# Routing attention and hardswish FFN on one core: decode intermediates in a PSUM bank, two banks for short-lived results, checks later

## The chip, the cores and the metric

The kernel runs on one core of a Trainium2 chip. Five engines work side by side, each on its own queue in program order: TensorE (PE, matrix products, with its weight loads in a row of their own, PEld), VectorE (DVE), ScalarE (ACT), GpSimd (POOL) and SyncE (SP, which issues transfers). The metric is device time in microseconds for one execution. Before the change three runs gave a median of 1086.1 us (1086.04 to 1087.46).

## The reference

Attention over 4 batches of 8 heads, 768 positions, 64 numbers per head, in which a query sees only keys of its own cluster (of 16), and then a feed-forward block with a hardswish.

```python
q_assign = np.argmax(np.einsum('bhsd,hcd->bhsc', q_n, c_n), axis=-1)   # nearest centroid
k_assign = np.argmax(np.einsum('bhsd,hcd->bhsc', k_n, c_n), axis=-1)
mask = q_assign[:, :, :, None] == k_assign[:, :, None, :]
scores = np.where(mask, scale * q @ k.T, -1e9)
attn = softmax(scores) @ v                       # (4, 8, 768, 64)
x = attn.transpose(0, 2, 1, 3).reshape(3072, 512)
h = x @ w_in                                     # (3072, 2048)
out = (h * np.clip(h + 3, 0, 6) / 6) @ w_out     # (3072, 512)
```

`w_in` and `w_out` come as 64-bit floats. The kernel turns them into 32-bit floats itself, from their two 32-bit words, in 32 chunks of 128 x 512.

## The kernel before

All work goes pair by pair: 16 pairs of heads, 12 steps n for each, two steps at a time. r is the place of such a double step in its pair (0, 2, ..., 10). Its engines' queues hold the instructions in the order of this loop:

```python
for n in range(0, total + lag_d + 2, 2):          # total = 192, lag_d = 4
    g, r = divmod(n, per_pair)                    # per_pair = 12
    scores(n), scores(n + 1)                      # PE ps, ACT ex, POOL acc
    attn_v(n - 2), attn_v(n - 1)                  # PE pv; at the end of a half: ACT num
    for check in later:                           # range passes and counts of the last double step
        check()
    later.clear()
    m = n - lag_d + 1
    if m >= 0 and m % NCH == NCH - 1:             # NCH = 6: at r = 2 and r = 8
        later.append(divide(m))
    prep = prep_items(g + 1, r)                   # next pair: r = 0, 2: two turns; 4: cluster_scores;
                                                  # 6: route; 8: two route_turns; 10: one
    if r == 4 and prep:
        prep.pop()()
    if n == DECODED:                              # DECODED = 96
        st["early"] = False
    ...                                           # loads, FFN items, mixed with prep one by one
    for step in decode[: share[r]]:               # share = {0: 5, 2: 3, 4: 4, 6: 1, 8: 3, 10: 4}
        step()
    del decode[: share[r]]
    ...
    if n >= total:
        for check in later:
            check()
        later.clear()
```

Short-lived results of PE (transposes, cluster scores, denominators) go to PSUM through `scratch`. Of the eight banks, `ps` has four, `pv` one, the pool `psum_t` one and the pool `psum_m` two. Up to n = 96 two of three such tiles go to `psum_m`, which the FFN's products `ph` share, and the third to `psum_t`; from n = 96 all go to `psum_t`.

```python
def scratch(shape, name):
    st["scratch"] += 1
    if st["early"] and st["scratch"] % 3:
        return psum_m.tile(shape, F32, name=name, tag="m")
    return psum_t.tile(shape, F32, name=name, tag="t")

def turn(g, part):
    ...
    pt = scratch([P, NHC, P], "pqk")              # three transposes of q or k
    ...
    nc.scalar.copy(out=dst, in_=pt)               # xf

def route_turn(g, part):
    ...
    po = scratch([P, 4, P], "po")
    ...
    nc.scalar.copy(out=xm[:, part * 4 : part * 4 + 4], in_=po)

def divide(n):
    ...
    pd = scratch([P, 512], "pd")[:, 0:HALF]       # denominators, from POOL's acc
    ...
    nc.vector.reciprocal(out=rcp, in_=pd)
    nc.vector.tensor_tensor(out=st["xT", b][...], in0=num, in1=rcp, op=ALU.mult)
    return lambda: in_range(2 * g + hf, rcp)

def in_range(i, rcp):                             # two passes of ACT with sums
    nc.scalar.activation(out=rcp, in_=rcp, func=ACT.Copy, accum_out=totals[:, 0, i : i + 1])
    nc.scalar.activation(out=rcp, in_=rcp, func=ACT.Relu, bias=low_c, scale=-1.0,
                         accum_out=totals[:, 1, i : i + 1])
```

`route` compares the transposed cluster scores `pr` with their maxima `mx` on DVE, giving `one_hot`, and appends a `count` (two ACT passes over `one_hot`) to `later`. `cluster_scores` writes `pcs`, which ACT copies to `cs`.

A chunk of weights is decoded in five steps; `lo` and `hi` are the two words, interleaved in SBUF. The tiles `wsize`, `wtop` and `wunit` are in SBUF, each twice.

```python
def split():
    load_weights(i + 1)
    ...
    nc.scalar.activation(out=got["size"], in_=got["hi"].bitcast(F32), func=ACT.Abs, accum_out=...)
    nc.vector.tensor_scalar(out=got["top"], in0=got["hi"], scalar1=3, scalar2=0x3FFFFFFF,
        op0=ALU.logical_shift_left, op1=ALU.bitwise_and)                     # wtop<-raw
def join():
    nc.vector.scalar_tensor_tensor(out=got["top"], in0=got["hi"], scalar=0xC0000000, in1=got["top"],
        op0=ALU.bitwise_and, op1=ALU.bitwise_or)                             # wtop<-raw,wtop
def power():
    nc.scalar.activation(out=got["size"], in_=got["size"], func=ACT.Relu, ..., accum_out=...)
    nc.vector.tensor_scalar(out=got["unit"], in0=got["top"], scalar1=0xFF800000, scalar2=None,
        op0=ALU.bitwise_and)                                                 # wunit<-wtop
def rest():
    nc.vector.scalar_tensor_tensor(out=unit, in0=got["lo"], scalar=2.0**-52, in1=unit,
        op0=ALU.mult, op1=ALU.mult)                                          # wunit<-raw,wunit
def total():
    nc.vector.tensor_tensor(out=chunks[i][0], in0=got["top"].bitcast(F32),
        in1=got["unit"].bitcast(F32), op=ALU.add)                            # w_in_sb<-wtop,wunit
```

Of the kernel before, what the change touches and what calls it, by code (L numbers as in the profile page):

```python
# [10 lines left out]
U32 = mybir.dt.uint32  # L11
# [7 lines left out]
P = 128  # L19
# [10 lines left out]
WC = 512  # L30
# [86 lines left out]
def fast_path(ctx, tc, ok, q, k, v, centroids, moe_w_in, moe_w_out, out):  # L117
# [6 lines left out]
    def pool(name, bufs, **kw):  # L124
        return ctx.enter_context(tc.tile_pool(name=name, bufs=bufs, **kw))
# [14 lines left out]
    decp = decoding.enter_context(tc.tile_pool(name="decp", bufs=2))  # L140
    psum_s = pool("psum_s", 2, space=PSUM)
    psum_v = pool("psum_v", 1, space=PSUM)
    psum_t = pool("psum_t", 1, space=PSUM)
# [17 lines left out]
    counts = const.tile([P, 2, NPAIR], F32, name="counts")  # L161
    w_low = const.tile([P, 1], F32, name="w_low")

    st = {"scratch": 0}
    later = []

    def scratch(shape, name):

        st["scratch"] += 1
        if st["early"] and st["scratch"] % 3:  # L170
            return psum_m.tile(shape, F32, name=name, tag="m")
        return psum_t.tile(shape, F32, name=name, tag="t")

# [2 lines left out]
    def load(g, *names):  # L176
        if g >= NPAIR:
            return
        b, h = divmod(2 * g, H)
        for name in names:  # L180
            if name == "v":
                dst = st["v", g] = vp.tile([P, NCH, 2, D], F32, name="vt")
            elif name == "q":
                st["qk", g] = qkp.tile([P, 2, NCH, 2, D], F32, name="qk")
            if name != "v":
                dst = st["qk", g][:, "qk".index(name)]
            src = {"q": q, "k": k, "v": v}[name]
            for t in range(2):
                nc.sync.dma_start(dst[:, :, t], src[b, h + t].rearrange("(p j) d -> p j d", p=P))
# [9 lines left out]
    def load_weights(i):  # L199
        if i < len(chunks):  # L200
            st["raw", i] = rawp.tile([P, WC, 2], U32, name="raw")
            nc.sync.dma_start(st["raw", i], chunks[i][1])

    def decoding_steps(i):

        got = {}

        def split():
            load_weights(i + 1)
            raw = st.pop(("raw", i))  # L210
            got.update(lo=raw[:, :, 0], hi=raw[:, :, 1])
            got["size"] = decp.tile([P, WC], BF16, name="wsize")
            got["top"] = decp.tile([P, WC], U32, name="wtop")
            got["unit"] = decp.tile([P, WC], U32, name="wunit")
            nc.scalar.activation(
                out=got["size"], in_=got["hi"].bitcast(F32), func=ACT.Abs,
                accum_out=w_totals[:, 0, i : i + 1],
            )
            nc.vector.tensor_scalar(  # L219
                out=got["top"], in0=got["hi"], scalar1=3, scalar2=0x3FFFFFFF,  # L220
                op0=ALU.logical_shift_left, op1=ALU.bitwise_and,
            )

        def join():
            nc.vector.scalar_tensor_tensor(
                out=got["top"], in0=got["hi"], scalar=0xC0000000, in1=got["top"],
                op0=ALU.bitwise_and, op1=ALU.bitwise_or,
            )

        def power():  # L230
            nc.scalar.activation(
                out=got["size"], in_=got["size"], func=ACT.Relu, bias=w_low, scale=-1.0,
                accum_out=w_totals[:, 1, i : i + 1],
            )
            nc.vector.tensor_scalar(
                out=got["unit"], in0=got["top"], scalar1=0xFF800000, scalar2=None, op0=ALU.bitwise_and
            )

        def rest():
            unit = got["unit"].bitcast(F32)  # L240
            nc.vector.scalar_tensor_tensor(  # L241
                out=unit, in0=got["lo"], scalar=2.0**-52, in1=unit, op0=ALU.mult, op1=ALU.mult
            )

        def total():
            nc.vector.tensor_tensor(  # L246
                out=chunks[i][0], in0=got["top"].bitcast(F32), in1=got["unit"].bitcast(F32), op=ALU.add
            )

        return [split, join, power, rest, total]  # L250


# [4 lines left out]
    def constants():  # L257
        make_identity(nc, ident)
        nc.vector.tensor_copy(out=ident_q, in_=ident)
        nc.vector.tensor_scalar_mul(out=ident_k, in0=ident, scalar1=-FAR)  # L260
        for t in range(2):
            nc.vector.tensor_reduce(
                out=parity[:, t : t + 1],
                in_=ident.rearrange("p (h t c) -> p t h c", t=2, c=C)[:, t], axis=AX.XY, op=ALU.max,
            )
        nc.gpsimd.memset(half_c, 0.5)
        nc.gpsimd.memset(low_c, 1.0 / BOUND)
        nc.gpsimd.memset(ones, 1.0)
        nc.gpsimd.memset(w_low, W_LOW)
        nc.gpsimd.memset(one_hot, 0.0)  # L270

    def centroid_norm():
        cn = unit_rows(nc, smallp, cen, D)

        nc.scalar.activation(out=w_totals[:, 0, 0:1], in_=w_low, func=ACT.Exp)

        wide = smallp.tile([P, 2, D], F32, name="cenwide")
        for t in range(2):
            nc.vector.tensor_scalar_mul(out=wide[:, t], in0=cn, scalar1=parity[:, t : t + 1])
        pc = scratch([P, P], "pc")  # L280
        nc.tensor.transpose(out=pc, in_=wide, identity=ident)
        nc.vector.tensor_copy(out=cnT, in_=pc)
# [5 lines left out]
    def turn(g, part):  # L288
        if part == 0:
            st["xf", g] = xp.tile([P, NC2, P], F32, name="xf")  # L290
        qk, xf = st["qk", g], st["xf", g]
        pt = scratch([P, NHC, P], "pqk")
        for i in range(NHC):
            j = part * NHC + i
            nc.tensor.transpose(out=pt[:, i], in_=qk[:, j // NCH, j % NCH], identity=ident)  # L295
        dst = xf[:, part * NHC : (part + 1) * NHC]
        nc.scalar.copy(out=dst, in_=pt)
        if part == 3:
            st.pop(("qk", g))
# [62 lines left out]
    def scores_qk(n):  # L362
        g, hf, j = where(n)
        st["ps", n] = psum_s.tile([P, 2, 512], F32, name="ps")
        scores_part(n, st["xf", g], True)
# [238 lines left out]
    total = NPAIR * per_pair  # L604
# [20 lines left out]
        return per_ffn + (n - END) * per_fast // per_batch  # L625

    st["early"] = True
    fill = []
    done = 0

    with tc.manual_schedule():
        nc.scalar.dma_start(cen, centroids.rearrange("h c d -> (h c) d"))
        load(0, "q", "k")
        constants()
        load(0, "v")
        load_weights(0)
        centroid_norm()
        for part in range(4):
            turn(0, part)
        load(1, "q", "k")  # L640
        scores_qk(0)
        scores_qk(1)
        cluster_scores(0)
        route(0)
        for part in range(3):
            route_turn(0, part)

        for n in range(0, total + lag_d + 2, 2):
            g, r = divmod(n, per_pair)
            for i in (n, n + 1):  # L650
                if i < total:
                    scores(i)
            for i in (n - lag_v, n - lag_v + 1):
                if 0 <= i < total:
                    attn_v(i)
            for check in later:
                check()
            later.clear()
            m = n - lag_d + 1
            if m >= 0 and m % NCH == NCH - 1:  # L660
                later.append(divide(m))
            prep = prep_items(g + 1, r)
            if r == 4 and prep:
                prep.pop()()
            if n == DECODED:
                st["early"] = False
            if m >= 0 and m % per_batch == per_batch - 1:
                fill += (fast_items if m >= per_batch else ffn_items)(m // per_batch)
            if r == 6:
                load(g + 2, "q", "k")  # L670
                load(g + 1, "v")
            want = items_by(n + 2) - done if n < total else len(fill)
            want = min(want, len(fill))
            done += want
            for i in range(max(len(prep), want)):
                if i < want:
                    fill.pop(0)()
                if i < len(prep):
                    prep[i]()
            for step in decode[: share[r]]:  # L680
                step()
            del decode[: share[r]]
            if n >= DECODED and (n - DECODED) // 2 < 8:
                weight_sums((n - DECODED) // 2)
            if n >= total:
                for check in later:
                    check()
                later.clear()

# [381 lines left out]
```

## Time and profile before

One profiled execution, span 1085.0 us:

| engine | busy us | share |
|---|---|---|
| PE | 1044.8 | 96% |
| PEld | 673.4 | 62% |
| DVE | 429.6 | 40% |
| ACT | 395.3 | 36% |
| POOL | 303.3 | 28% |

The shares are means over stages of different kinds. In a line of the profile "L219 DVE TENSOR_SCALAR wtop<-raw" names the line of the kernel, the engine, the operation and what it writes from what it reads. A wait line gives who waited for whom: us in total, times, the longest. A timeline line gives start, length, and in square brackets how long the engine stood idle before it and what ended that.

### The profile page before, as it was taken

The page shows a single profiled execution, that of the slowest core. Times are in us where ns is not written, and L with a number is a line of the kernel's source. Part 1 is how long each engine was busy: PE and PEld are TensorE (multiplying, and loading weights), DVE is VectorE, ACT ScalarE, POOL GpSimd, SP SyncE. Part 2 cuts the span into 40 slices and gives each one's busy share as a digit, 9 for nine tenths or more (in the row PEclk, how much of TensorE's full clock was granted, in tenths as well). Part 3 has the DMA queues.
Part 4 walks back from the last instruction along what each step waited for, and adds up shares of the span by engine and source line. Part 5 has one row for each costly group of instructions (what it writes and reads, how often), then busy time and mean ns, then how long its engine had stood idle before and what let it go on. Part 6 is the DMA issues. An engine that isn't in the chain of part 4 may idle for free.

```text
span 1085.0 us, 12781 instructions
## 1 busy us (share of the span) xinstructions
PE 1044.8 (96%) x5218; PEld 673.4 (62%) x5218; DVE 429.6 (40%) x609; ACT 395.3 (36%) x798; POOL 303.3 (28%) x171
## 2 busy tenths in 40 slices
PE   6988889999999999999999999999999999999997
PEld 3433344444445544776677667676667678888886
DVE  5888897678312202421331321332232141413141
ACT  6777666666301301333432442432242330102010
POOL 3756565464310101323231322322322320000000
PEclk9989899999999999999999999999999999999999
DMA  5444442434002000020200202020100000000000
GB/s 146 95 106 111 102 111 70 102 86 119 1 19 54 1 10 20 1 44 21 44 1 1 63 1 44 21 44 1 34 1 1 20 1 1 21 20 1 20 1 24
DMA packets 83540, 42.89 MB, mean 40 GB/s; under 512 B 76304, under 2 KB 76304, under 8 KB 83472
## 3 DMA queue, kind: packets, MB, share of 16 engines
q1 hardware_dynamic: 83328, 41.95, 15.1%
q8 instruction: 43, 0.70, 0.3%
q14 instruction: 25, 0.20, 0.1%
q10 hardware_dynamic: 144, 0.03, 0.0%
HBM read 35.68 MB, written 6.29 MB: 39 GB/s over the span
## 4 chain that ended last, share of the span: by engine, by line
PE 88%; DVE 7%; ACT 2%; issue 1%; DMA 1%; POOL 0%; DVEq 0%; POOLq 0%; ACTq 0%; SPq 0%
PE ph L521 24%; PE ps L371 13%; PE Y L539 12%; PE pv L400 10%; PE X L539 9%; PE py L474 8%; PE ph L457 7%; DVE rcp L425 2%; PE pd L421 2%; PE pqk L295 2%; DVE w_in_sb L246 1%; DVE wunit L241 1%; DVE wtop L219 1%; PE pcs L308 1%; PE po L351 1%
## 5 line engine op out<-in xcount | busy, mean ns | idle before, releaser
L390 POOL TENSOR_TENSOR acc<-acc,ex 128x768 f32<-128x768 f32 x128 | 240.9, 1882 | 399.3 <-ACT ex L383 394.3
L521 PE MATMUL ph<-xT,w_in_sb 128*128 128x256 f32 x1152 | 259.6, 382 | 0.0
L521 PEld LDWEIGHTS ph<-xT,w_in_sb 128*128 128x128 f32 x1152 | 215.3, 190 | 46.2 <-issue 18.1
L383 ACT ACTIVATE ex<-ps 128x768 f32<-128x768 f32 x192 | 150.2, 807 | 139.5 <-PE ps L371 139.0
L444 ACT ACTIVATE g_sb<-ph,half_c 128x512 f32<-128x512 f32 (+1 forms) x104 | 68.1, 654 | 313.6 <-PE ph L521 245.8
L445 DVE SCALAR_TENSOR_TENSOR g_sb<-g_sb,ph 128x512 f32<-128x512 f32 (+1 forms) x104 | 67.2, 646 | 279.6 <-ACT g_sb L444 279.5
L371 PE MATMUL ps<-xf 64*128 64x384 f32 x768 | 170.2, 522 | 4.2 <-ACT ex L383 4.2
L400 PE MATMUL pv<-ex,vt 128*64 128x384 f32 x768 | 146.1, 502 | 0.0
L425 DVE RECIPROCAL rcp<-pd 128x384 f32<-128x384 f32 x32 | 81.8, 2555 | 81.2 <-PE pd L421 81.2
L387 POOL TENSOR_TENSOR acc<-ex 128x768 f32<-128x768 f32 x32 | 60.2, 1883 | 183.9 <-ACT ex L383 183.6
L400 PEld LDWEIGHTS pv<-ex,vt 128*64 128x64 f32 x768 | 46.9, 137 | 81.8 <-issue 77.1
L371 PEld LDWEIGHTS ps<-xf 64*128 64x128 f32 x768 | 64.9, 191 | 52.2 <-issue 30.9
L457 PE MATMUL ph<-xT,w_in_sb 128*128 128x384 f32 x256 | 87.3, 493 | 1.6 <-DVE rcp L425 1.6
L474 PE MATMUL py<-w_out_sb,g_sb 128*128 128x512 f32 x192 | 84.0, 594 | 0.0
L457 PEld LDWEIGHTS ph<-xT,w_in_sb 128*128 128x128 f32 x256 | 47.2, 190 | 41.1 <-issue 6.7
L539 PE MATMUL Y<-w_out_sb,g_sb 128*128 128x256 f32 x288 | 66.1, 383 | 0.0
L546 DVE TENSOR_TENSOR y<-y,Y 128x256 f32<-128x256 f32 x36 | 15.1, 420 | 127.2 <-PE Y L539 126.6
L539 PE MATMUL Y<-T,g_sb 128*128 128x256 f32 x288 | 65.3, 380 | 0.0
L539 PE MATMUL X<-w_out_sb,g_sb 128*128 128x256 f32 x288 | 65.3, 380 | 0.0
L371 PE MATMUL ps<-xm 64*128 64x384 bf16 x384 | 64.4, 330 | 0.3 <-ACT xm L355 0.3
L474 PEld LDWEIGHTS py<-w_out_sb,g_sb 128*128 128x128 f32 x192 | 35.9, 190 | 44.2 <-issue 43.3
L539 PEld LDWEIGHTS Y<-w_out_sb,g_sb 128*128 128x128 f32 x288 | 53.9, 190 | 12.9 <-issue 6.0
(88 smaller groups left out, 833.9 us busy)
## 6 DMA issues: line engine op xcount, KB each, us to landing
raw<-in_moe_w_in_dram SPq DMA_DIRECT2D x16, 512.0 KB, 3.7
raw<-in_moe_w_out_dram SPq DMA_DIRECT2D x16, 512.0 KB, 3.6
qk<-in_q_dram SPq DMA_DIRECT2D x32, 192.0 KB, 4.1
qk<-in_k_dram SPq DMA_DIRECT2D x32, 192.0 KB, 4.2
vt<-in_v_dram SPq DMA_DIRECT2D x32, 192.0 KB, 4.2
out_dram<-y SPq DMA_DIRECT2D x24, 256.0 KB, 2.1
cen<-in_centroids_dram ACTq DMA_DIRECT2D x1, 32.0 KB, 1.7
```

The costliest lines, as they stand in the source:

```text
L371: nc.tensor.matmul(st["ps", n][:, t, 0:HALF], lhsT=x[r, NCH + j], rhs=x[r, hf * NHC : (hf + 1) * NHC], start=first, stop=not first,)
L383: nc.scalar.activation(out=ex, in_=sc, func=ACT.Exp, scale=SM_SCALE)
L387: nc.gpsimd.tensor_tensor(out=acc, in0=st["ex", n - 1], in1=ex, op=ALU.add)
L390: nc.gpsimd.tensor_tensor(out=acc, in0=acc, in1=ex, op=ALU.add)
L400: nc.tensor.matmul(pv[t * D : (t + 1) * D], lhsT=vt[:, j, t], rhs=ex[:, t], start=(j == 0), stop=(j == NCH - 1),)
L425: nc.vector.reciprocal(out=rcp, in_=pd)
L444: nc.scalar.activation(out=g, in_=h, func=ACT.Relu, bias=half_c, scale=1.0 / 6.0)
L445: nc.vector.scalar_tensor_tensor(out=g, in0=g, scalar=1.0, in1=h, op0=ALU.min, op1=ALU.mult)
L457: nc.tensor.matmul(hh, lhsT=w_in_sb[:, kt, f * P : (f + 1) * P], rhs=xT[:, kt, hf * HALF : (hf + 1) * HALF], start=(kt == 0), stop=(kt == ...
L474: nc.tensor.matmul(py, lhsT=st["g", f][:, i * P : (i + 1) * P], rhs=w_out_sb[:, f], start=(f == 0), stop=(f == NFT - 1),)
L521: nc.tensor.matmul(ph[:, t * HC : (t + 1) * HC], lhsT=w_in_sb[:, kt, f * P : (f + 1) * P], rhs=xT[:, kt, 2 * m * P : 2 * (m + 1) * P], sta ...
L539: nc.tensor.matmul(bank[:, half * HC : (half + 1) * HC], lhsT=g_sb[:, kind, i], rhs=w[:, i], start=(first and i == 0), stop=(last and i == ...
```

## The change

The decode step's tile `wtop`, which holds the sign, exponent and leading bits of a chunk, moves from SBUF to the PSUM bank of `psum_t`, once and not twice. It is meant to keep VectorE and GpSimd out of each other's way at SBUF. That bank is then no longer free for short-lived results, which have the two banks of `psum_m` alone up to n = 96. And the range passes (`in_range`) and tie counts (`count`) go from the middle of the next double step to its end, where they don't stand ahead of ScalarE's copies.

```diff
-    st = {"scratch": 0}
+    st = {}
     later = []

     def scratch(shape, name):

-        st["scratch"] += 1
-        if st["early"] and st["scratch"] % 3:
+        if st["early"]:
             return psum_m.tile(shape, F32, name=name, tag="m")
         return psum_t.tile(shape, F32, name=name, tag="t")
...
             got["size"] = decp.tile([P, WC], BF16, name="wsize")
-            got["top"] = decp.tile([P, WC], U32, name="wtop")
+            got["top"] = psum_t.tile([P, WC], U32, name="wtop", tag="t")
             got["unit"] = decp.tile([P, WC], U32, name="wunit")
...
-    fill = []
+    fill, checks = [], []
...
-            for check in later:
-                check()
-            later.clear()
             m = n - lag_d + 1
             if m >= 0 and m % NCH == NCH - 1:
                 later.append(divide(m))
...
-            if n >= total:
-                for check in later:
-                    check()
-                later.clear()
+            for check in checks:
+                check()
+            checks, later[:] = later[:], []
+
+        for check in checks:
+            check()
```

## The prediction

> **What bounds the kernel now.** I began with the page. Its 40 slices (27.1 us each) are read as tenths of busy time.
>
> ```profile
> PE   6988889999999999999999999999999999999997
> DVE  5888897678312202421331321332232141413141
> POOL 3756565464310101323231322322322320000000
> PEclk9989899999999999999999999999999999999999
> ```
>
> TensorE (PE) is full from slice 7 on. Only in slices 1 to 6 is there room: PE at 8 tenths, its clock down at times, VectorE (DVE) at 8 to 9. The changed code runs in just this stretch: weights are decoded in double steps n = 0 to 94, which end near 285 us. So I cut it into stretches, one for each pair of heads (from a pair's first `pqk` transposes to the next pair's). The columns are: stretch, length, busy us with counts in brackets, clock, DMA share and GB/s.
>
> ```profile
> 17.60:41.90 24.30, 24.30 (x161) 11.14 (x159) 18.21 (x16) 22.48 (x51) 19.21 (x10) 0.98 0.43 100
> 41.90:74.85 32.95, 27.64 (x166) 12.14 (x164) 28.46 (x28) 22.34 (x51) 19.53 (x10) 0.90 0.40 100
> 74.85:106.10 31.25, 26.44 (x166) 11.58 (x164) 27.62 (x28) 22.30 (x50) 20.06 (x10) 0.95 0.39 106
> 106.10:137.80 31.70, 26.69 (x165) 11.73 (x163) 27.24 (x28) 22.53 (x50) 19.81 (x10) 0.89 0.42 106
> 137.80:174.65 36.85, 32.95 (x190) 15.66 (x189) 35.13 (x35) 23.66 (x54) 21.25 (x11) 1.00 0.42 109
> ```
>
> The first pair takes 24.30 us with PE always busy. The next three do nearly the same work (one more `divide`, 0.67 us of PE) and take 32 us. This is what can be won. The list of waits says who holds PE up in 30 to 160 us:
>
> ```profile
> ACT rcp L433 <- DVE xT L426: 18.2, 4, 5.0
> PE pr L319 <- ACT cs L313: 7.3, 2, 4.1
> PE pcs L308 <- DVE rcp L425: 5.0, 1, 5.0
> PE ps L371 <- ACT ex L383: 4.2, 6, 0.8
> ```
>
> Four times ScalarE (ACT) stands up to 5 us at the first pass of `in_range`, which waits for `xT`; PE waits behind it for copies and exponentials. The root is that DVE is late. Lines from the timeline of one case:
>
> ```profile
> 45.87 0.81 PE L421 MATMUL pd<-acc,ones 128*64 128x384 f32 x4
> 46.17 4.03 POOL L390 TENSOR_TENSOR acc<-acc,ex 128x768 f32<-128x768 f32 x2 [2.20 <-ACT ex L383]
> 46.21 2.32 DVE L246 TENSOR_TENSOR w_in_sb<-wtop,wunit 128x512 f32<-128x512 f32 x1
> 48.45 2.03 DVE L219 TENSOR_SCALAR wtop<-raw 128x512 uint32<-128x512 uint32 x1
> 54.67 2.54 DVE L425 RECIPROCAL rcp<-pd 128x384 f32<-128x384 f32 x1
> 57.91 0.52 ACT L433 ACTIVATE rcp<-rcp 128x384 f32<-128x384 f32 x1 [4.96 <-DVE xT L426]
> 59.68 0.90 PE L319 MATMUL pr<-ident,cs 128*128 128x128 f32 x3 [4.05 <-ACT cs L313]
> ```
>
> `pd` was done at 46.68, but its reciprocal starts 8 us later, behind six decode instructions. Three of them take 2.32, 2.03 and 2.32 us, where their shortest records are 0.69 and 0.41: they lie beside GpSimd (POOL) adds and end only after them. The groups of that window (30 to 160 us) give the size:
>
> ```profile
> L246 DVE TENSOR_TENSOR w_in_sb<-wtop,wunit 128x512 f32<-128x512 f32 x14 | 22.0, 1571 | 0.5
> L219 DVE TENSOR_SCALAR wtop<-raw 128x512 uint32<-128x512 uint32 x16 | 19.6, 1227 | 0.0
> L241 DVE SCALAR_TENSOR_TENSOR wunit<-raw,wunit 128x512 f32<-128x512 uint32 x16 | 17.5, 1096 | 0.4
> ```
>
> [...] Those with a PSUM operand never stretch: `rcp<-pd` 2.544 to 2.559 us in 32, `one_hot<-pr,mx` 0.347 to 0.359 in 32, the gate on `ph` at most 0.690. Those in SBUF alone do: `xT` 0.557 to 1.397, the five decode steps 0.41 to 2.34. [...] 512 elements take 0.42 us from SBUF to SBUF (`wtop`, `wunit`), and 0.692 for the copy `y<-py` out of PSUM. [...] after the 4.05 us wait the four `ps` products take 1.65 us in place of 0.92.
>
> **Part 1: `wtop` in PSUM.** An instruction is added or removed nowhere; four of the five steps change their operands. [...] `join` and `total` keep one SBUF input. I take 0.69 us for each, from `y<-py` and the gate; no record shows VectorE writing PSUM, so that half is an estimate. `rest` has both inputs in SBUF still and meets POOL alone: 0.69 plus the chance that POOL is busy (81.5 of 130 us, 0.63) times half an add (0.95) is 1.29. A chunk then takes 4 x 0.69 + 1.29 = 4.05 us. Before, in 30 to 160 us, it took 5.18 (the five groups' 82.9 us over 16 chunks). So 1.13 us per chunk, 4.5 per pair. DVE per pair falls from 27.8 to 23.3 us. As one `wtop` ends in `total` before the next begins in `split`, on the same engine, a single bank adds no wait.
>
> A pair of PE work without waits is 24.3 + 0.67 = 25.0 us, and a little less at full clock (0.98 there): 24.6. With DVE at 23.3 and ACT at 22.4 the pair can be bound by PE again. Following DVE's queue from one reciprocal to the next, with r for the place in the pair: after that of r = 8 come `xT` and 12 decode steps (3.2 + 10.3 us); PE comes to the next `pd` after some 12.7 us. The reciprocal is then about 1 us late and not 8, too little to hold up ACT one double step later. Three engines above 90% in fixed order will not fit perfectly; I choose 1.5 us per pair for that.
>
> **Part 2: checks later.** The two passes of `in_range` and their sums (1.3 us of ACT) and the counts (1.1) move from ahead of the copies to the end of the double step. This removes no work. It takes the head-of-line wait in front of `cs`. With part 1 done there is little of that wait left, so I count no gain twice. Late in the kernel the waits for such copies are 3.7 us in all (`po` 2.1, `pqk` 1.6 after 430 us); perhaps 0.5 comes off.
>
> **Part 3: two banks in place of three.** This costs. In a double step with `pd`, two more short-lived tiles follow at once. Does the second wait for the reciprocal (2.56 us), or for ScalarE's copy of the first? Counting the tiles in the code, the `pd` at 78.8 us is the 34th and `pcs` at 83.6 the 37th; both fall to the two-bank pool, with `pqk` (35th) between. `pcs` ran at 83.61 without waiting, while the reciprocal ran only from 85.93. So the pool gave it the bank of `pqk`, freed by ACT, and not the one of `pd`. In the next pair `pd` and `pcs` are the 45th and 48th, both in the single bank, and `pcs` waited the 5.0 us in the list above. I therefore count an ACT copy: 0.48 (`xf`) or 0.56 (`xm`) plus some 0.1, about 0.6 us, twice per pair (r = 2 and 8). Where an FFN product `ph` stands ahead of the two `pqk` of r = 0, a third time.
>
> **The sum.** Pairs 1 to 3: 95.9 us before; 3 x (24.6 + 1.2 + 1.5) = 81.9 after; gain 14.0. Pair 4 has three `ph` of 2.75 us: 24.6 + 8.3 + 1.2 + 0.7 = 34.8 against 36.85; gain 2.0. Pair 0 and the start: loss 0.9. Pairs 5 to 7 (to 285 us) have DVE to spare and PE nearly full: 3 x 1.7 = 5.1 lost, of which the present waits (0.9, 0.9 and 0.7) give 1 back; loss 4. Late: gain 0.5. In all 14.0 + 2.0 - 0.9 - 4.0 + 0.5 = 11.6: 1086.1 - 11.6 = 1074.5 us, rounded to 1075.
>
> **Rivals.**
> A, two banks bind: if the second tile waits for the reciprocal, each place costs 2.3 us in place of 0.6; the 10 places without a `ph` between (two in each of pairs 1 to 3, one in pairs 0 and 4, two after 160 us) would then cost 17 us more, and the gain is gone: 1092. For it: `po` waited 0.9 us on `rcp` once (164.6 us). Against it: the `pcs` above.
> B, [...] DVE's freed time is taken by longer `rest` steps, or in-place work in one PSUM bank is slower than 0.69. At 5 us a chunk nothing is gained early and the 5 us of bank waits stay: 1088.
> C, all of it comes off: PE idles 18.1 us in 30 to 160 and runs 7% slow in clock there (8 us more). If all 26 went and the bank waits hid behind other work: 1060.
>
> **Range and chances.** 1064 to 1088 holds most of C at one end and B at the other; A lies outside. Faster by over 2% needs under 1064.4, 22 of C's 26 us: 0.10. Slower by over 2% needs over 1107.8, more than A: 0.02. Within 2%: 0.88.
>
> **What would show it.** In the changed profile: `split`, `join`, `power`, `total` flat near 0.69 with no record near 2 us, `rest` near 1.3; pairs 1 to 3 near 27 us with the clock at 1.0; no wait of ACT `rcp` on `xT` over 2 us; new PE waits of about 0.6 us at the second `pqk` and `po`, released by ACT. It is wrong if those waits are released by `rcp` and last over 2 us, if the PSUM writes take over 1 us, or if ACT becomes the engine PE waits for in each pair.

## The result and the profile after

The changed kernel takes 1073.4 us (median of 4, 1072.7 to 1073.9), the kernel before beside it 1086.8. The ratio is 0.987 (95% interval 0.984 to 0.990): 13.4 us less. The prediction was 1075, with 1064 to 1088 as its range.

The 40 slices of the changed kernel (26.8 us each), as before:

```profile
PE   6999999999999999999999999999999999999997
DVE  5788865565122103420331331332231232314141
POOL 3777644444011002223223222323232320000000
PEclk9999999999999999999999999999999999999999
```

TensorE is full from slice 1 on, and its clock no longer drops (9 tenths in all 40 slices). VectorE, at 8 to 9 tenths in slices 1 to 5 before, is there only in slices 2 to 4. Cut at the first `pqk` of each pair (the busy columns, here and in the prediction, are PE, PEld, DVE, ACT and POOL):

```profile
16.64:41.49 24.85, 24.18 (x161) 10.81 (x159) 16.13 (x22) 21.92 (x52) 18.15 (x10) 1.00 0.46 113
41.49:67.70 26.21, 24.97 (x166) 11.09 (x164) 22.32 (x28) 22.14 (x52) 18.50 (x10) 1.00 0.51 126
67.70:93.91 26.21, 24.97 (x166) 11.08 (x164) 22.74 (x28) 22.12 (x52) 18.51 (x10) 1.00 0.48 126
93.91:120.12 26.21, 24.97 (x166) 11.08 (x164) 22.75 (x28) 22.12 (x52) 18.51 (x10) 1.00 0.50 126
```

Pairs 1 to 3 take 26.21 us each, all alike, where they took 32.95, 31.25 and 31.70. The groups of VectorE in 30 to 160 us show why:

```profile
L240 DVE SCALAR_TENSOR_TENSOR wunit<-raw,wunit 128x512 f32<-128x512 uint32 x19 | 20.2, 1065 | 0.5
L234 DVE TENSOR_SCALAR wunit<-wtop 128x512 uint32<-128x512 uint32 x19 | 13.1, 688 | 0.5
L224 DVE SCALAR_TENSOR_TENSOR wtop<-raw,wtop 128x512 uint32<-128x512 uint32 x18 | 12.6, 699 | 0.6
L218 DVE TENSOR_SCALAR wtop<-raw 128x512 uint32<-128x512 uint32 x18 | 12.5, 694 | 0.4
L245 DVE TENSOR_TENSOR w_in_sb<-wtop,wunit 128x512 f32<-128x512 f32 x14 | 9.7, 691 | 0.5
```

Four steps are flat at 0.69 us; their longest record in the whole trace is 0.749. Only `rest` (`wunit<-raw,wunit`), with both inputs in SBUF, still stretches, to 1.07 on average. A chunk costs 0.694 + 0.699 + 0.688 + 1.065 + 0.691 = 3.84 us. Of the kernel before, beside the rows that the prediction shows, the same window has:

```profile
L225 DVE SCALAR_TENSOR_TENSOR wtop<-raw,wtop 128x512 uint32<-128x512 uint32 x16 | 12.6, 786 | 0.6
L235 DVE TENSOR_SCALAR wunit<-wtop 128x512 uint32<-128x512 uint32 x16 | 8.2, 513 | 0.4
L246 DVE TENSOR_TENSOR w_out_sb<-wtop,wunit 128x512 f32<-128x512 f32 x2 | 3.0, 1514 | 0.1
```

With those rows that is 82.9 us for 16 chunks, 5.18 each. What came in the place of the lateness is in the timeline of a double step with `pd`:

```profile
71.66 0.82 PE L420 MATMUL pd<-acc,ones 128*64 128x384 f32 x4
72.41 0.55 PE L294 MATMUL pqk<-ident,qk 128*128 128x128 f32 x3
72.59 2.56 DVE L424 RECIPROCAL rcp<-pd 128x384 f32<-128x384 f32 x1
72.99 0.48 ACT L296 COPY xf<-pqk 128x384 f32<-128x384 f32 x1 [0.48 <-PE pqk L294]
73.53 0.55 PE L294 MATMUL pqk<-ident,qk 128*128 128x128 f32 x3 [0.57 <-ACT xf L296]
```

The reciprocal now starts as soon as `pd` is done, here and in all nine cases between 30 and 160 us; before, it came 6 to 8 us late in four of eight. The six `pqk` transposes, one run before, are now split into two groups: the second waits 0.57 us for ScalarE's copy of the first, and not for the reciprocal, which runs to 75.1. In each pair a group of `po` waits in the same way, here in pair 1:

```profile
60.54 0.27 PE L350 MATMUL po<-ident_q,one_hot 128*128 128x128 bf16 x2 [0.67 <-ACT xm L354]
```

From the list of TensorE's waits in the first 285 us:

```profile
PE po L350 <- ACT xm L354: 6.3, 9, 0.9
PE pqk L294 <- ACT xf L296: 6.2, 10, 0.7
```

ScalarE's own list for these 285 us has no wait on `xT` left.

Stage by stage, from cuts of both traces at the first `pqk` of a pair:

| stage | before, us | after, us | measured | predicted |
|---|---|---|---|---|
| start and pair 0 | 41.91 | 41.49 | -0.4 | +0.9 |
| pairs 1 to 3 | 95.90 | 78.63 | -17.3 | -14.0 |
| pair 4 | 36.84 | 34.43 | -2.4 | -2.0 |
| pairs 5 to 7 | 114.07 | 120.36 | +6.3 | +4.0 |
| rest | 796.28 | 796.39 | +0.1 | -0.5 |
| span | 1085.0 | 1071.3 | -13.7 | -11.6 |

### The profile page after: what moved, and what is told of

Read it like the earlier page. It is cut to its first block, busy times and chain, and to the rows that moved or that the text cites. A ratio compares the mean times of both kernels' runs of the same rounds, so it can differ in the third digit from the quotient of the medians.

```text
span 1071.3 us, 12819 instructions
## 1 busy us (share of the span) xinstructions
PE 1039.3 (97%) x5218; PEld 670.0 (63%) x5218; DVE 394.1 (37%) x609; ACT 391.2 (37%) x798; POOL 294.1 (27%) x171
## 4 chain that ended last, share of the span: by engine, by line
PE 97%; ACT 2%; DVE 1%; issue 0%; POOL 0%; POOLq 0%; DVEq 0%
PE ph L520 24%; PE ps L370 16%; PE pv L399 13%; PE Y L538 12%; PE X L538 9%; PE ph L456 8%; PE py L473 8%; PE pqk L294 2%; PE pd L420 2%; PE pcs L307 1%; PE po L350 1%; ACT g_sb L443 1%; ACT xm L354 1%; PE pr L318 1%; ACT xf L296 0%
## 5 line engine op out<-in xcount | busy, mean ns | idle before, releaser
L389 POOL TENSOR_TENSOR acc<-acc,ex 128x768 f32<-128x768 f32 x128 | 233.9, 1828 | 398.3 <-ACT ex L382 392.9
L370 PE MATMUL ps<-xf 64*128 64x384 f32 x768 | 165.8, 510 | 0.0
L386 POOL TENSOR_TENSOR acc<-ex 128x768 f32<-128x768 f32 x32 | 58.0, 1813 | 180.4 <-ACT ex L382 180.4
```

Of the source, the lines that this page charges most:

```text
L370: nc.tensor.matmul(st["ps", n][:, t, 0:HALF], lhsT=x[r, NCH + j], rhs=x[r, hf * NHC : (hf + 1) * NHC], start=first, stop=not first,)
L386: nc.gpsimd.tensor_tensor(out=acc, in0=st["ex", n - 1], in1=ex, op=ALU.add)
L389: nc.gpsimd.tensor_tensor(out=acc, in0=acc, in1=ex, op=ALU.add)
```

## The experiments

**The theory.** VectorE is late because its decode steps wait out GpSimd's adds. In the kernel before all their operands are in SBUF; the shortest record of each of the five steps is 0.41 to 0.69 us, the longest, beside an add, 2.02 to 2.34. ScalarE and TensorE queue behind it. `wtop` in PSUM ends that for the four steps that use it. The two banks cost TensorE about 0.6 us per place, and the later checks add nothing once VectorE is in time. **The rivals:** ScalarE's order is the cause; VectorE has simply too many instructions; the bank waits hide elsewhere.

### The checks alone

```diff
 (the kernel before; ahead of divide)
-            for check in later:
-                check()
-            later.clear()
 ... (at the end of the double step)
+            for check in checks:
+                check()
+            checks, later[:] = later[:], []
```

> Only the range passes and counts move to the end of the double step; wtop stays in SBUF, three banks stay. My theory (VectorE is late because its decode steps wait out GpSimd's adds): [...] VectorE is still some 8 us late once per pair, but ScalarE now meets the wait behind its copies, so part of the stall goes: 1077 to 1084 us. Rival (the whole gain comes from ScalarE's order): about 1073. Rival (the order is worth nothing): 1086.

Measured: 1083.2 us, ratio 0.997 (0.996 to 0.998), 3.6 us less (2 to 4 by the interval) where the change has 13.4. The list of waits in 30 to 160 us:

```profile
ACT wsize L215 <- DMA raw<-in_moe_w_in_dram: 13.5, 7, 2.8
PE ps L371 <- ACT ex L383: 9.3, 6, 2.9
PE pcs L308 <- DVE rcp L425: 5.6, 1, 5.6
ACT rcp L433 <- DVE xT L426: 0.6, 2, 0.3
```

The wait on `xT` is nearly gone (18.2 us before), and most of the time is not. VectorE is still late: its five steps reach 1.9 to 2.35 us as before, the reciprocal of pair 1 starts 6 us after its `pd`, and VectorE is busy 88.3 of the 94.2 us of pairs 1 to 3. ScalarE now waits for the next raw chunk, whose transfer in turn waits for `rest`, VectorE's last reader of the buffer (17 waits, 103.1 us in this window), and TensorE waits for ScalarE's exponentials. The order moved the wait; it was not its source.

### `wtop` in PSUM with two banks, checks as before

```diff
 (the kernel before)
-            got["top"] = decp.tile([P, WC], U32, name="wtop")
+            got["top"] = psum_t.tile([P, WC], U32, name="wtop", tag="t")
-        st["scratch"] += 1
-        if st["early"] and st["scratch"] % 3:
+        if st["early"]:
```

> Only wtop moves to PSUM, with two banks for short-lived results; the checks stay where they were. My theory: nearly the whole gain, 1073 to 1077 us, with no wait of ScalarE's range pass on xT over 2 us. Rival (ScalarE's order gives the gain): 1083 or more.

Measured: 1073.8 us, ratio 0.990 (0.988 to 0.992); the profiled span is 1071.5 us against 1071.3 of the full change. A window of pair 2:

```profile
67.96:94.17 26.21, 24.97 (x166) 11.08 (x164) 22.22 (x28) 22.31 (x50) 18.82 (x11) 1.00 0.50 126
```

It is the same 26.2 us per pair, and ScalarE has no listed wait on `xT`. On top of this part, the later checks are worth nothing that these runs resolve.

### Two banks alone

```diff
 (the kernel before)
-        st["scratch"] += 1
-        if st["early"] and st["scratch"] % 3:
+        if st["early"]:
```

> Only the third bank is taken away: short-lived results go to two banks up to n = 96, the third stays empty, wtop in SBUF, checks as before. My theory: some 20 waits of about 0.6 us for ScalarE's copies come, partly beside stalls that are there already: 1090 to 1097 us. Rival (the waits hide elsewhere): 1086 to 1088.

Measured: 1091.7 us, ratio 1.006 (1.004 to 1.008). From the list of waits, 0 to 290 us:

```profile
PE pr L318 <- ACT cs L312: 8.3, 4, 3.1
PE pqk L294 <- ACT xf L296: 6.2, 10, 0.7
PE po L350 <- ACT xm L354: 6.1, 9, 0.9
```

Nearly the same bank waits as in the changed kernel (12.3 us, 12.5 there), but only 4.9 us more time: in pairs 1 to 3 they lie beside stalls that VectorE causes anyway (95.2 us for the three, against 95.9). So what the banks cost depends on what else is late.

### GpSimd's adds taken away

This kernel leaves out the sums of the denominators but for one step's (plus one), so its output is another; GpSimd keeps one instruction per half, and everything else is as before.

```diff
 (the kernel before)
-            nc.gpsimd.tensor_tensor(out=acc, in0=st["ex", n - 1], in1=ex, op=ALU.add)
-        elif j > 1:
-            acc = st["acc", g, hf]
-            nc.gpsimd.tensor_tensor(out=acc, in0=acc, in1=ex, op=ALU.add)
+            nc.gpsimd.tensor_scalar(
+                out=acc, in0=ex, scalar1=1.0, scalar2=1.0, op0=ALU.mult, op1=ALU.add
+            )
```

> The kernel before, but GpSimd makes one instruction per half (acc = ex + 1) in place of five adds: the denominators are left out but for one step's, so only the time counts. wtop in SBUF, three banks, checks as before. My theory: without GpSimd's adds the decode steps fall to 0.42 and 0.69 us, VectorE is in time, and with three banks there are no bank waits: 1059 to 1066 us. Rival (VectorE is late by the number of its instructions[...]): 1080 or more.

Measured: 1060.1 us, ratio 0.977 (0.976 to 0.979). Groups of VectorE in 30 to 160 us, and the window of pair 2:

```profile
L225 DVE SCALAR_TENSOR_TENSOR wtop<-raw,wtop 128x512 uint32<-128x512 uint32 x19 | 13.2, 693 | 0.7
L241 DVE SCALAR_TENSOR_TENSOR wunit<-raw,wunit 128x512 f32<-128x512 uint32 x19 | 13.1, 691 | 0.5
L219 DVE TENSOR_SCALAR wtop<-raw 128x512 uint32<-128x512 uint32 x19 | 10.0, 528 | 0.3
L235 DVE TENSOR_SCALAR wunit<-wtop 128x512 uint32<-128x512 uint32 x20 | 8.5, 424 | 0.5
```

```profile
66.12:90.70 24.58, 24.58 (x166) 11.05 (x164) 19.16 (x28) 22.12 (x50) 1.70 (x2) 1.00 0.53 134
```

With the same number of VectorE instructions, `wtop` in SBUF and the checks in their old place, VectorE is in time: 19.2 us per pair in place of 27.8, and TensorE never waits in pairs 1 to 3. In this window only `split` is above its 0.42 us: once per pair it lies beside the one GpSimd instruction left and takes 0.85 to 1.03. The lateness is GpSimd's doing, not that of the instruction count. 24.58 us is also the pair without any wait that the prediction put at 24.6.

### The other tile in PSUM

```diff
 (the changed kernel)
-            got["top"] = psum_t.tile([P, WC], U32, name="wtop", tag="t")
-            got["unit"] = decp.tile([P, WC], U32, name="wunit")
+            got["top"] = decp.tile([P, WC], U32, name="wtop")
+            got["unit"] = psum_t.tile([P, WC], U32, name="wunit", tag="t")
```

> The changed kernel with wunit in the PSUM bank and wtop back in SBUF, twice. By my theory [...] the held ones are now split (0.42 us alone) and join (0.69), while power, rest and total stay flat near 0.69 us: VectorE per chunk about 0.7 us over the changed kernel at most, still in time, so 1073 to 1079 us. Rival (what counts is that fewer bytes move in SBUF, not which operands an instruction has): all five stretch alike or none does.

Measured: 1074.2 us, ratio 0.987 (0.985 to 0.988), the same as the change. The durations (shortest, median, longest, in ns) of the tile `wtop` and then of `wunit`:

```profile
L218 DVE TENSOR_SCALAR wtop<-raw x32: 418/421/2066, 14.8 to 262.9; 128x512 uint32<-128x512 uint32 x32
L224 DVE SCALAR_TENSOR_TENSOR wtop<-raw,wtop x32: 684/694/2203, 15.3 to 269.1; 128x512 uint32<-128x512 uint32 x32
...
L234 DVE TENSOR_SCALAR wunit<-wtop x32: 682/695/696, 16.0 to 269.9; 128x512 uint32<-128x512 uint32 x32
L240 DVE SCALAR_TENSOR_TENSOR wunit<-raw,wunit x32: 687/695/721, 16.7 to 270.7; 128x512 f32<-128x512 uint32 x32
```

The stretched instructions have changed places: `split` and `join` reach 2.1 and 2.2 us, `rest` is flat (0.72 at most). In this run as in the change, the steps that stretch are those with all their operands in SBUF, and those with one in PSUM stay at 0.75 us or less. So what counted here is each instruction's own operands, and not how much moves in SBUF.

### `pd` between the two tiles

```diff
 (the changed kernel; the order within a double step)
-            if m >= 0 and m % NCH == NCH - 1:
+            due = m >= 0 and m % NCH == NCH - 1
+            if due and not (st["early"] and n < DECODED and g + 1 < NPAIR):
                 later.append(divide(m))
+                due = False
 ...
             for i in range(max(len(prep), want)):
-                if i < want:
+                if n >= DECODED and i < want:
                     fill.pop(0)()
                 if i < len(prep):
                     prep[i]()
+                if due:
+                    later.append(divide(m))
+                    due = False
+                if n < DECODED and i < want:
+                    fill.pop(0)()
```

> The changed kernel with another order up to n = 96: the denominators' product pd stands between the two short-lived tiles of its double step, not ahead of them, and an FFN item stands behind a transpose group, not ahead of it. So ScalarE's copy of the first tile lies beside 0.67 us of TensorE work. My theory (the two banks cost TensorE 12.1 us of waits on ScalarE's copies): most of the waits go, 1061 to 1065 us. Rival (they hide other waits that then appear): 1070 to 1073.

Measured: 1062.0 us, ratio 0.975 (0.973 to 0.978): better than both kernels. The timeline of TensorE in pair 1, and the window of pair 2:

```profile
45.99 0.55 PE L294 MATMUL pqk<-ident,qk 128*128 128x128 f32 x3
46.47 0.87 PE L420 MATMUL pd<-acc,ones 128*64 128x384 f32 x4
47.27 0.55 PE L294 MATMUL pqk<-ident,qk 128*128 128x128 f32 x3
```

```profile
67.07:92.22 25.15, 25.15 (x166) 10.86 (x164) 22.89 (x28) 22.05 (x52) 18.92 (x11) 1.00 0.48 132
```

ScalarE's copy lies beside `pd`, and from 16 to 290 us TensorE has no listed wait at all. So with the same two banks another order of work is worth some 11 us (1071.3 against 1060.4 by span). Two things moved. Pairs 1 to 3 hold no FFN item, so there the new place of `pd` alone brings 3.2 us (78.63 to 75.43); the gain in pairs 4 to 7, some 8 us, is not parted between the two. With its groups still split, a pair takes 0.57 us more than the 24.58 us of the run without GpSimd's adds, which has three banks.

### The two banks strictly in turn

```diff
 (the changed kernel)
-    psum_m = pool("psum_m", 2, space=PSUM)
+    psum_m0 = pool("psum_m0", 1, space=PSUM)
+    psum_m1 = pool("psum_m1", 1, space=PSUM)
+
+    class InTurn:
+        n = 0
+
+        def tile(self, *args, **kw):
+            self.n += 1
+            return (psum_m0, psum_m1)[self.n % 2].tile(*args, **kw)
+
+    psum_m = InTurn()
```

> The changed kernel with the two banks given out strictly in turn (two pools of one bank each). Then the second short-lived tile behind pd takes pd's bank and waits for the reciprocal (2.56 us) and not for ScalarE's copy. My theory: some 10 places cost 1.7 us more each: 1086 to 1093 us, with TensorE's waits released by rcp. Rival (the banks were given in turn already, or the wait hides): 1072 to 1075.

Measured: 1101.5 us, ratio 1.011 (1.009 to 1.014), 8.5 us above what I expected at most. From the list of TensorE's waits up to 290 us, its timeline, and the windows of pairs 1 and 2:

```profile
PE po L360 <- DVE rcp L434: 11.9, 5, 2.4
PE pqk L304 <- DVE rcp L434: 11.2, 5, 2.3
```

```profile
66.93 0.40 PE L360 MATMUL po<-ident_q,one_hot 128*128 128x128 bf16 x4
69.72 0.27 PE L360 MATMUL po<-ident_q,one_hot 128*128 128x128 bf16 x2 [2.40 <-DVE rcp L434]
...
70.04 0.92 PE L380 MATMUL ps<-xf 64*128 64x384 f32 x4
...
71.06 1.49 PE L380 MATMUL ps<-xf 64*128 64x384 f32 x4
```

```profile
45.63:78.52 32.89, 28.24 (x166) 12.18 (x164) 22.22 (x29) 22.36 (x52) 18.74 (x10) 0.90 0.40 103
78.52:109.77 31.25, 26.60 (x165) 11.59 (x164) 22.11 (x28) 22.25 (x52) 18.58 (x10) 0.95 0.42 106
```

The waits are as foreseen: ten on `rcp`, 23.1 us. With seven on VectorE's product `g_sb` in the FFN (6.4 us), TensorE's waits up to 290 us grow by 17.4 us over the change, and by 1.0 later. What I had left out is the clock: TensorE's busy time grows by 10.6 us (1049.9 against 1039.3), of which 1.0 lies before the first of these waits. Together that is the 28.9 us between the two spans (1100.2 and 1071.3). This is rival A of the prediction, and it would have made the change slower than the kernel before.

## Why the prediction was right

**Part 1, the stretched steps.** Right in kind: two experiments with different operands (`wtop` or `wunit` in PSUM) and one without most of GpSimd's adds agree. They show which steps stretch beside an add, not what in the hardware holds them up. Sizes: the four steps with `wtop` in PSUM are 0.69 us as estimated, also the two in which VectorE writes PSUM, which no record had shown; `rest` is 1.07 and not 1.29, so a chunk is 3.84 and not 4.05 us, and VectorE per pair about 22.6 and not 23.3.

**The fit of three engines.** This is the term of the sum that was mis-sized: I put 1.5 us per pair on it. A changed pair is 26.21 us; less 24.58 (the run without GpSimd's adds) that is 1.63, of which the two listed bank waits are 0.57 + 0.67. The other 0.4 is TensorE time that I had not counted: six transposes take 0.87 in one go and 0.55 + 0.55 in two. Nothing is left for the fit; queues with 22 of 26 us busy did run side by side, and the reciprocal that I had put 1 us late starts 0.1 to 0.2 us after its `pd`. Over pairs 1 to 3 the term is 4.5 us too high, and the split groups give 1.2 of that back: an error of 3.3 us.

**Part 2, the checks.** That no gain be counted twice was right; the 0.5 us late in the kernel did not come (796.28 and 796.39): the 3.7 us of waits for copies there are the same in both.

**Part 3, the banks.** The choice that mattered was which bank the second tile takes. The reading of the trace before (`pcs` not waiting where the reciprocal had not yet run) held: ScalarE's copies release all 19 listed waits for a bank, and the in-turn run shows what the other answer would have cost. The size was low in pairs 5 to 7: 6.3 us, not 4.0. The nine waits there come to 6.3 us by the timeline against 1.6 before, of which I had credited 1 (one of the three waits that I named lies in pair 4), and each split group costs TensorE 0.2 us more.

**The total.** It is nearer than its terms. Pairs 1 to 4 gained 3.7 us more than predicted and the start and pair 0 came out 1.3 better, pairs 5 to 7 lost 2.3 more and late in the kernel 0.6 was missing; that leaves 2.1. Most of the 1.3 is luck of the two profiles: up to the first `pqk` of pair 0 TensorE's clock was 0.93 before and 1.00 after (9.16 and 8.03 us busy for the same 48 products), which hides the loss of 0.9 that was predicted. One reading of the prediction was loose: TensorE is at 8 tenths in slices 2 to 5 only; 1 and 6 are at 9.

**Rivals.** A failed on the bank, B on the flat 0.69; C's 1060 is what the kernels nearly without bank waits reach (1060.1, 1062.0), and the change itself loses the difference to the split groups and their waits.

## What to carry to other kernels

If an engine's instruction has a median far under its mean, ask which other engine's instructions it ends with (here `wtop<-raw`: a median of 0.42 us, a mean of 0.93). Where others wait for the late engine, try one operand in the other memory even if the instruction alone then takes longer: here two steps of 0.42 us became 0.69, and the chunk fell from 5.18 to 3.84. A copy that frees a bank should lie beside other work of the engine that wants the bank: a new order of `pd` and the FFN items within their double step was worth nearly as much as the whole change (some 11 us). And a wait can cost more than its length: in the in-turn run a drop of TensorE's clock added some 1.6 us to a wait of 2.3 (an estimate: the other 9.6 us of busy time over six drops).

## What was not expected

Of the ten waits of 2.2 to 2.4 us on `rcp` in the in-turn run, six are followed by 3 to 4 us in which TensorE's products take nearly twice their time: four `ps` products 1.49 us in place of 0.81, sometimes from the first product on, once (in the timeline above) only 1 us after the wait. After the other four nothing changes:

```profile
86.03 0.55 PE L304 MATMUL pqk<-ident,qk 128*128 128x128 f32 x3 [2.25 <-DVE rcp L434]
86.50 0.92 PE L380 MATMUL ps<-xf 64*128 64x384 f32 x4
```

A pair with two such drops has a mean granted clock of 0.90, a pair with one 0.95; the waits of 0.6 to 0.9 us in the changed kernel leave it at 1.00. All ten are shorter than the 4.05 us wait after which the prediction read slow `ps` products in the kernel before. What tells the six from the four no run shows. In pairs 1 to 3 of the kernel before, the same loss came with the stalls: TensorE's busy time there, at a granted clock of 0.89 to 0.95, was 80.8 us; in the changed kernel, at 1.00, it is 74.9 with no product removed.
